# New tables of due times for the planner that orders a fused attention and two-layer feed-forward kernel

## The chip, the cores and the metric

The kernel runs on one core of a Trainium2 chip. The metric is the device time of one execution in microseconds (us), the median of the runs; less is better.

## The reference

Causal attention with a decay bias, then a gated feed-forward layer behind an RMS norm, then a second feed-forward layer, all in fp32. B = 4, H = 8 (32 heads), S = 576, D = 64, 2304 tokens of width 512, inner widths 1536 and 2048.

```python
def _attn_ref(q, k, v, s):
    scores = scale * np.matmul(q, k.transpose(0, 1, 3, 2))
    cum = np.cumsum(np.maximum(s, 0.0), axis=-1)
    bias = -(cum[:, :, :, None] - cum[:, :, None, :])
    scores = np.where(causal, -1000000000.0, scores + np.minimum(bias, 0.0))
    attn = np.exp(scores - np.max(scores, axis=-1, keepdims=True))
    attn = attn / (np.sum(attn, axis=-1, keepdims=True) + 1e-09)
    return np.matmul(attn, v)
...
    # _moe_ref
    xn = x / np.sqrt(np.mean(x * x, axis=-1, keepdims=True) + 1e-06) * rms_g
    g = xn @ w_gate
    return g * (1.0 / (1.0 + np.exp(-g))) * (xn @ w_val) @ w_out
...
    # _moe2_ref
    h = x @ w_in
    return h * (1.0 / (1.0 + np.exp(-1.702 * h))) @ w_out
```

## The kernel before

**Stages.** The attention stage works head by head. `scores(h, u)` is TensorE's product of queries and keys, in five units u; for each block VectorE adds the mask and takes a running minimum (a custom instruction, written to a tile `PA`), and `expo` is ScalarE's exponential with the row sum. `recip` and `norm` divide by the sum (the five `norm` instructions of a head run on GpSimd). `transp(h, t)` is TensorE's transposes of the head, in four runs of 3 or 4, each into one of only two PSUM banks and copied from there by ScalarE or VectorE. `pv(h, piece)` is the product with the values for two heads at once. After the eight heads of a batch, `rms(b)` takes the sums of squares, VectorE works on them in twelve small instructions, and `scale(b, half)` spreads the result by three transposes into a PSUM bank, from where VectorE multiplies it into the tile `xT` in four instructions.

Heads 0 to 13 are multiplied in fp32. Heads 14 to 31 are split into a rounded part and a remainder: for these, `prep` loads Q and K of two heads (two DMAs of 288 KB), rounds, subtracts, and copies the parts to their places by six SBUF-to-SBUF DMAs of 144 KB per head, and two rows of the cumulative bias by one DMA from `ch_d`. All DMAs are issued by SyncE, in one queue.

Into the attention stage two of the twelve inner chunks of the first feed-forward layer are mixed as filler: `fa_tile(j)`, j = 0 to 3, each with 16 groups `gv` of three matmuls (128x384) and four groups `outp` of six. Then comes the **chain**: the rest of both feed-forward layers, by Strassen-like block products, as one chain of TensorE operations of fixed order. The tiles share slots of SBUF by turns; the slot `sd` holds the filler's `FH` first and the chain's block `B21` afterwards, so `B21` can be written only once the last `outp` has read `FH`.

**What sets the order.** Nothing is issued where the code names it. Every operation is recorded with its inputs, outputs and possible engines (`op(eng, fn, ...)`, "AV" for ScalarE or VectorE, "VG" for VectorE or GpSimd). A planner then places all operations: it keeps a model of each engine, takes for each engine the ready operations, and among those the one with the smallest latest start (`alap`). The latest starts are reckoned back from the chain, whose ideal start is the number `TA`, and from due times out of the table `PRM`: `SD` (one number per head for its scores), `HD` (one per pair of heads for `pv`), `FD` (first and last for each filler tile) and `WD` (one for each of the first six weights). They are priorities and not times of day. The planner also picks the engine where there is a choice. The instructions are issued in the order of its starts, and each engine keeps that order (a dependency without a semaphore). Where GpSimd takes an instruction that shares a port with VectorE, it is also made to wait for VectorE's last such instruction.

```python
pick = None
for i in ready[e]:
    t, c = earliest(e, i)
    if t <= tnow and (pick is None or (alap[i], i) < (alap[pick[1]], pick[1])):
        pick = (t, i, c)
```

Since a recording helper issues everything, all rows of the profile show line 211; tiles tell them apart. In the profile's names, `b` is a PSUM bank, `si`, `sk` and some `s` are the `PA` tiles, `sf`, `sg`, `sh` and `sb` the copied transposes, `st` raw weights, and `small` the minima, sums and reciprocals.

Of the kernel before, what the change touches and what calls it, by code (L numbers as in the profile page):

```python
# [39 lines left out]
    "RQ": "AVG", "RV": "VG", "NORM": "G",  # L40
    "SJ": [(2, (2, 3)), (2, (4,)), (1, (2, 3, 4)), (0, (3, 4, 5)), (0, (6, 7)), (1, (5, 6, 7)), (2, (5, 6, 7)),
           (2, (8, 9)), (1, (8, 9)), (0, (8, 9)), (0, (10, 11)), (1, (10, 11)), (2, (10, 11))],
    "HD": [16.92, 309.44, 401.69, 409.67, 394.22, 578.63, 529.92, 440.48, 0.0, 29.27, 423.83, 579.22, 136.47, 502.33, 517.43, 246.34],
    "FD": [(20.84, 419.25), (430.11, 416.77), (419.39, 381.61), (573.39, 343.22)],
    "WD": [636.01, 275.43, 695.53, 257.09, 229.42, 237.34],
    "SD": [331.83, 393.3, 216.64, 633.04, 341.05, 237.85, 481.65, 585.57, 647.63, 420.68, 664.9, 112.11, 264.2, 413.34, 130.04, 443.31, 550.66, 141.32, 470.11, 462.61, 149.18, 360.93, 387.56, 358.59, 700.0, 456.49, 215.88, 71.5, 280.43, 357.78, 664.75, 190.27],
    "TA": 257.35, "REB": 3, "EARLY": False, "MAG": "AV", "PASS": 0, "ISSUE": 0.6, "INNER": 1.0, "IDLE": 3, "PEN": {}, "PVC": (0.81, 2.22),
}


# [1419 lines left out]
```

## Time and profile before

| | |
|---|---|
| median of 3 runs | 1006.09 us (1004.43 to 1006.52) |
| profiled execution | 1007.22 us, span of its profile 1005.4 us |
| TensorE busy | 990.2 us (98%) |
| VectorE, ScalarE, GpSimd busy | 657.4 us (65%), 562.5 us (56%), 272.2 us (27%) |
| TensorE's granted clock | 0.999 of full |

The share of busy time counts a TensorE instruction from its start to its modelled end. The idle time of TensorE is what no instruction covers, and the profile names what released it.

### The profile page before, as it was taken

To read this page: it belongs to the slowest core of one execution; us is meant where nothing else is said; L and a number is where in the kernel's file an instruction comes from. 1 tells how busy PE (TensorE), PEld (TensorE's weight loads), DVE (VectorE), ACT (ScalarE), POOL (GpSimd) and SP (SyncE) were. 2 spreads that over 40 slices of the span, in tenths; PEclk is the share of its full clock that TensorE was granted. 3 is DMA by queue.
4 is the path that set the end of the run, shared out by engine and by line. 5 is a ranking of instruction groups with operands and counts; after the bars stand their busy time and mean duration, and the time that the engine had idled before them with its cause. 6 is when DMAs were issued, how large, how long until landed. Compare 5 with 4: busy or idle time off the path is not lost. (4 is left out here: it accounts for less than half of the span.)

```text
span 1005.4 us, 16237 instructions
## 1 busy us (share of the span) xinstructions
PE 990.2 (98%) x5738; PEld 907.1 (90%) x5738; DVE 657.4 (65%) x1524; ACT 562.5 (56%) x1292; POOL 272.2 (27%) x370
## 2 busy tenths in 40 slices
PE   9999999899999999999999999999999999999998
PEld 6777878789899999999999999999889998899987
DVE  7778786877868887645766858874653565353323
ACT  8999777685566555334444436785643463353322
POOL 5555652442232223002321303231320231020000
PEclk9999999999999999999999999999999999999999
DMA  5347787733676772661484576653276046505541
GB/s 170 96 131 183 192 223 201 178 101 118 251 244 242 267 271 87 260 218 45 132 319 174 209 293 234 275 198 146 88 299 220 22 157 238 192 1 194 212 160 63
DMA packets 62089, 183.49 MB, mean 182 GB/s; under 512 B 7092, under 2 KB 22964, under 8 KB 62008
## 3 DMA queue, kind: packets, MB, share of 16 engines
q1 hardware_dynamic: 62008, 182.46, 53.5%
q8 instruction: 45, 0.74, 0.3%
q14 instruction: 36, 0.29, 0.1%
HBM read 122.32 MB, written 44.19 MB: 166 GB/s over the span
## 5 line engine op out<-in xcount | busy, mean ns | idle before, releaser
L211 ACT ACTIVATE s<-b 128x384 f32<-128x384 f32 (+1 forms) x267 | 127.3, 489 | 145.0 <-PE b L211 82.3
L211 DVE TENSOR_TENSOR xT<-b,xT 128x384 f32<-128x384 f32 (+1 forms) x158 | 92.5, 599 | 87.5 <-PE b L211 86.7
L211 ACT ACTIVATE b<-b 128x384 f32<-128x384 f32 x125 | 58.3, 479 | 107.7 <-DVE b L211 72.3
L211 POOL TENSOR_TENSOR wa<-wa,st 128x512 int32<-128x512 int32 x50 | 66.0, 1319 | 176.0 <-DVE wa L211 83.2
L211 DVE TENSOR_TENSOR s<-b,s 128x384 fp32r<-128x384 f32 (+1 forms) x121 | 66.4, 553 | 68.5 <-ACT s L211 64.1
L211 PE MATMUL b<-s,w 128*128 128x384 f32 x540 | 107.5, 335 | 1.0 <-ACT s L211 0.5
L211 PE MATMUL b<-s 128*128 128x288 f32 (+11 forms) x420 | 101.1, 364 | 4.4 <-DVE small L211 2.2
L211 PEld LDWEIGHTS b<-s,w 128*128 128x128 f32 x540 | 94.9, 188 | 2.8 <-DVE s L211 1.4
L211 PEld LDWEIGHTS b<-s 128*128 128x128 f32 (+1 forms) x420 | 67.1, 192 | 17.7 <-issue 5.3
L211 DVE TENSOR_TENSOR b<-b,s 128x384 f32<-128x384 f32 x82 | 46.1, 562 | 51.6 <-PE b L211 44.0
L211 POOL TENSOR_SCALAR wm<-wm 128x512 f32<-128x512 f32 x68 | 41.8, 615 | 139.6 <-DVE wm L211 46.1
L211 ACT ACTIVATE s<-s,small 128x576 f32<-128x576 f32 (+4 forms) x100 | 55.2, 554 | 13.7 <-DVE small L211 13.1
L211 POOL TENSOR_SCALAR s<-s,small 128x448 f32<-128x448 f32 (+4 forms) x100 | 51.6, 535 | 38.9 <-DVE wm L211 13.9
L211 PE MATMUL b<-sc,w 128*128 128x384 f32 x300 | 61.3, 341 | 0.0
L211 ACT ACTIVATE st<-st 128x512 int32<-128x512 uint32 x68 | 45.8, 674 | 23.7 <-DMA st<-in_w_dram 23.7
L211 PE MATMUL b<-s,s 128*128 128x384 f32 (+1 forms) x252 | 54.9, 346 | 0.0
L211 PE MATMUL b<-sd,w 128*128 128x384 f32 x264 | 52.4, 336 | 0.0
L211 PEld LDWEIGHTS b<-sc,w 128*128 128x128 f32 x300 | 51.4, 188 | 0.3
L211 PE MATMUL b<-w,s 128*128 128x512 f32 x189 | 51.1, 391 | 0.0
L211 PE MATMUL b<-s,sk 128*128 128x384 f32 x246 | 50.7, 335 | 0.0
L211 DVE CUSTOM_DVE_ANT_0 s<-b,s 128x288 f32<-128x288 f32 (+4 forms) x100 | 39.8, 426 | 11.8 <-PE b L211 11.4
L211 PE MATMUL b<-s,sc 128*128 128x384 f32 x228 | 47.2, 334 | 0.0
(265 smaller groups left out, 2375.7 us busy)
## 6 DMA issues: line engine op xcount, KB each, us to landing
st<-in_w_dram SPq DMA_DIRECT2D x68, 512.0 KB
s<-s SPq DMA_DIRECT2D x108, 144.0 KB
xT<-y_d SPq DMA_DIRECT2D x3, 1536.0 KB
s<-pc11B SPq DMA_DIRECT2D x6, 768.0 KB
s<-pc21B SPq DMA_DIRECT2D x6, 768.0 KB
out_dram<-xT SPq DMA_DIRECT2D x18, 256.0 KB
y_d<-se SPq DMA_DIRECT2D x22, 192.0 KB
s<-in_vp_dram SPq DMA_DIRECT2D x16, 256.0 KB
```

The costliest lines, as they stand in the source:

```text
L211: return lambda *args, **kw: f(*[real(x) for x in args], **{k: real(x) for k, x in kw.items()})
```

## The change

Five entries of `PRM` get other numbers: `HD`, `FD`, `WD`, `SD` and `TA`. No code, no tile, no cost of the planner's model and no other entry is changed. One short line of the tables and the line with `TA`:

```diff
-    "WD": [636.01, 275.43, 695.53, 257.09, 229.42, 237.34],
+    "WD": [258.65, 630.56, 454.31, 104.08, 19.12, 583.8],
...
-    "TA": 257.35, "REB": 3, "EARLY": False, "MAG": "AV", "PASS": 0, "ISSUE": 0.6, "INNER": 1.0, "IDLE": 3, "PEN": {}, "PVC": (0.81, 2.22),
+    "TA": 229.72, "REB": 3, "EARLY": False, "MAG": "AV", "PASS": 0, "ISSUE": 0.6, "INNER": 1.0, "IDLE": 3, "PEN": {}, "PVC": (0.81, 2.22),
```

What this does to the order is seen in the built programs. TensorE's operations before the chain stand in another order almost throughout; the order of the chain's own operations is the same, and behind the last norm the rows of all TensorE instructions read alike.

The first place is TensorE at the end of the attention stage: the last filler products (`outp`, tile `sd` by `w`), the transposes of the last norm's first half (`ident,small`), and the chain's products on `B21` (the first tile `sd` by `sl`). Before:

```order
L211 MATMUL b_72<-sd_1339,w_130 128x384 x3
L211 MATMUL b_73<-sd_1339,w_127 128x384 x3
L211 MATMUL b_73<-sd_1339,w_130 128x384 x3
L211 MATMUL b_70<-ident,small 128x128 x2
L211 MATMUL b_70<-ident,small 128x64
L211 MATMUL b_66<-sd_2903,sl_2676 128x384 x6
```

Now:

```order
L211 MATMUL b_73<-sd_1396,w_127 128x384 x3
L211 MATMUL b_73<-sd_1396,w_130 128x384 x3
L211 MATMUL b_67<-s_1_2611,sk_2646 128x384 x6
L211 MATMUL b_70<-ident,small 128x128 x2
L211 MATMUL b_70<-ident,small 128x64
L211 MATMUL b_66<-sd_2882,sl_2735 128x384 x6
```

Six matmuls of the chain (on `sk`) that stood ahead of the filler products now stand behind the last of them.

The second place is SyncE's queue ahead of the scores of head 25: its last part copies (`s_0_928` and `s_0_234`, now `s_0_897` and `s_0_232`, from `s_0_136`), its bias rows (`ch_d`), and the loads of heads 26 and 27 (`in_qT_dram`, `in_kT_dram`). Before:

```order
L211 DMA s_0_928<-s_0_136 64x576 x4
L211 DMA s_0_136<-in_qT_dram 128x576
L211 DMA s_0_928<-s_0_136 64x576
L211 DMA s_0_136<-in_kT_dram 128x576
L211 DMA s_0_234<-s_0_136 64x576
L211 DMA s_0_234<-ch_d 2x576
L211 DMA s_0_149<-in_vp_dram 128x4x128
```

Now:

```order
L211 DMA s_0_897<-s_0_136 64x576 x3
L211 DMA s_0_232<-s_0_136 64x576
L211 DMA s_0_232<-ch_d 2x576
L211 DMA s_0_136<-in_qT_dram 128x576
L211 DMA s_0_136<-in_kT_dram 128x576
L211 DMA y_d<-se_1328 128x384 x2
```

The two loads stood among the copies and ahead of the bias rows; now they stand behind them.

The third place is TensorE around the norm of batch 2: transposes of heads 25 (`s_0_159`), 26 (`s_0_165`) and 27 (`s_0_131`, now), filler (`w`), and the norm's own transposes (`ident,small`; the rows with `x2` and the 64 behind it are the first half, the next three the second). Before:

```order
L211 MATMUL b_69<-ident,s_0_159 128x128 x4
L211 MATMUL b_70<-ident,small 128x128 x2
L211 MATMUL b_70<-ident,small 128x64
L211 MATMUL b_68<-ident,s_0_159 128x128 x4
L211 MATMUL b_69<-ident,s_0_159 128x128 x3
L211 MATMUL b_73<-sc_915,w_129 128x384 x6
L211 MATMUL b_70<-ident,small 128x64
L211 MATMUL b_70<-ident,small 128x128
L211 MATMUL b_70<-ident,small 128x64
L211 MATMUL b_68<-ident,s_0_165 128x128 x4
```

Now:

```order
L211 MATMUL b_68<-ident,s_0_165 128x128 x4
L211 MATMUL b_70<-ident,small 128x128 x2
L211 MATMUL b_70<-ident,small 128x64
L211 MATMUL b_69<-ident,s_0_165 128x128 x3
L211 MATMUL b_73<-sc_925,w_129 128x384 x3
L211 MATMUL b_72<-sc_925,w_128 128x384 x3
L211 MATMUL b_69<-ident,s_0_131 128x128 x4
L211 MATMUL b_68<-ident,s_0_131 128x128 x4
L211 MATMUL b_70<-ident,small 128x64
L211 MATMUL b_70<-ident,small 128x128
L211 MATMUL b_70<-ident,small 128x64
L211 MATMUL b_71<-s_0_897 128x192
```

Head 26's transposes began right behind the second half of the norm; now all but the last run stand ahead of the first half, and two runs of head 27 stand between the halves.

The planner's choice of engine changes too. In the whole program GpSimd gets 13 more two-input instructions (four of 128x576, four of 128x384, three of 128x512, one each of 128x768 and 128x256) and 8 more of 128x5. These 13 leave VectorE, with five one-input roundings and masks; VectorE gets six more copies of 128x448 and one of 128x256 out of PSUM.

## Rows read from the trace of the kernel before

**Rows 1.** The page's head.
```profile
span 1005.4 us, 16237 instructions
```

**Rows 2.** Five stretches: us, then busy us (and instructions) of each engine, clock, DMA.
```profile
0.00:248.00 248.00, 239.94 (x1708) 195.89 (x1709) 191.45 (x663) 197.75 (x562) 123.26 (x225) 1.00 0.59 157
248.00:270.00 22.00, 19.81 (x108) 18.03 (x107) 19.64 (x46) 13.14 (x23) 3.21 (x3) 1.00 0.66 248
270.00:600.00 330.00, 329.07 (x1893) 327.62 (x1893) 230.85 (x439) 159.15 (x317) 78.24 (x77) 1.00 0.59 212
600.00:1000.00 400.00, 399.76 (x2029) 364.60 (x2028) 214.76 (x378) 192.42 (x392) 67.52 (x65) 1.00 0.46 172
1000.00:1005.40 5.40, 1.60 (x8) 0.98 (x6) 0.69 (x1) 0.00 (x0) 0.00 (x0) 0.87 0.26 97
```

**Rows 3.** TensorE's waits from 0 to 270 us: total us, times, longest us.
```profile
PE b L211 <- DVE small L211: 2.2, 4, 1.4
PE b L211 <- POOL s L211: 1.4, 2, 1.3
PE b L211 <- DMA s<-ch_d: 1.4, 1, 1.4
PE b L211 <- DVE xT L211: 0.8, 2, 0.5
PE b L211 <- DVE sg L211: 0.8, 1, 0.8
PE b L211 <- POOL si L211: 0.7, 1, 0.7
PE b L211 <- ACT sd L211: 0.6, 1, 0.6
PE b L211 <- DVE sd L211: 0.5, 1, 0.5
PE b L211 <- DMA s<-s: 0.4, 2, 0.2
PE b L211 <- ACT s L211: 0.4, 1, 0.4
PE b L211 <- DVE sf L211: 0.3, 1, 0.3
PE b L211 <- ACT sg L211: 0.3, 1, 0.3
PE b L211 <- ACT sf L211: 0.2, 1, 0.2
```

**Rows 4.** Timeline at the chain's first products on `sd`: TensorE, ScalarE, VectorE.
```profile
254.84 0.45 PE L211 MATMUL b<-sd,sl 128*128 128x384 f32 x1 [0.57 <-ACT sd L211]
255.83 1.14 PE L211 MATMUL b<-sd,sl 128*128 128x384 f32 x5 [0.55 <-DVE sd L211]
253.94 0.84 ACT L211 ACTIVATE sd<-xT 128x768 fp32r<-128x768 f32 x1 [1.13 <-PE b L211]
254.82 0.96 DVE L211 TENSOR_TENSOR sd<-xT,sd 128x768 fp32r<-128x768 f32 x1
```

**Rows 5.** Timeline of SyncE's queue and TensorE at the scores of head 25.
```profile
162.41 0.54 SPq L211 DMA_DIRECT2D s<-in_qT_dram  x1
...
165.18 0.44 SPq L211 DMA_DIRECT2D s<-ch_d  x1
169.49 1.28 PE L211 MATMUL b<-s 128*128 128x192 f32 x7 [1.43 <-DMA s<-ch_d]
```

**Rows 6.** Timeline of TensorE around the norm of batch 2.
```profile
186.77 0.72 PE L211 MATMUL b<-ident,small 64*128 64x64 f32 x3 [0.51 <-DVE xT L211]
188.76 0.66 PE L211 MATMUL b<-ident,s 128*128 128x128 f32 x4 [1.27 <-POOL s L211]
```

**Rows 7.** Instruction groups from 0 to 250 us: busy us, mean ns.
```profile
L211 POOL TENSOR_TENSOR s<-s 128x576 fp32r<-128x576 f32 x4 | 5.7, 1427 | 5.8 <-DMA st<-in_w_dram 3.5 <-ACT small L211 1.4 <-DVE s L211 0.7
...
L211 DVE TENSOR_TENSOR s<-s 128x576 fp32r<-128x576 f32 x14 | 10.4, 758 | 0.0
```

6 rows, old and new, of the table PRM are left out of this document.

## The prediction

> **What bounds the kernel now.** I read the five stretches first [rows 2]: the granted clock is at its full level (2.4 GHz) in the first four and TensorE is busy nearly throughout. Against the span [rows 1] it is idle for 15.2 us: 8.06 us before 248 us (248.00 - 239.94), 2.19 us to 270 us, 0.93 us to 600 us, 0.24 us to 1000 us, 3.80 us behind that. So TensorE's work is the bound, and another order can give back no more than its idle time. The chain's order is the same in both programs; what lies behind 270 us (4.97 us idle) I leave as it is. The field is the 10.25 us before 270 us.
>
> TensorE's waits in that stretch [rows 3] tell what ends them; the rows add up to 10.0 us. Not all is to be had. The first wait of all, for VectorE's setup (the longest in the first row, 1.4 us), is there in either order. So are the two for `sg` (0.8 + 0.3 us): that block comes from the last norm's second half, and between the two stand the same rows in both orders. This leaves 7.5 us.
>
> **The change, part by part.** The work is the same: the same matmuls, transposes and DMAs. What a term is worth is a wait that the new order takes apart, less what it puts there.
>
> *Filler's end.* `B21` waits for the last filler product to have read the shared slot. ScalarE's half starts at 253.94 us, when TensorE is done with it, and ends at 254.78; VectorE's half runs from 254.82 to 255.78 us, and both halves are waited for, 0.57 + 0.55 us [rows 4]. The new order puts six matmuls of 128x384 between the last filler product and `B21`'s product. One such matmul takes 329.07 / 1893 = 0.174 us in the dense stretch [rows 2], six take 1.04 us. The first product then comes at 254.27 + 1.04 = 255.31 us, behind ScalarE's half; the second, 0.17 us later, meets VectorE's half at 255.83 us and waits 0.35 us. Gain 1.12 - 0.35 = **0.8 us** (0 to 1.1).
>
> *Head 18.* Its transposes wait for GpSimd's division (`si`, 0.7 us) and then run four runs on end through two banks, so that one more waits for ScalarE's copy (`sf`, 0.2 us) [rows 3]. Before, between its last score and its first transposes stood the scores of head 19, one piece of `pv` and two filler groups. In the new order five filler groups of three matmuls (5 x 3 x 0.174 = 2.6 us), two runs and more of other heads' transposes, the norm's second half, the same scores and a shorter piece of `pv` stand there, and two filler products and a piece of `pv` among the runs. The three filler groups more (1.6 us) and the transposes outweigh the longer piece of `pv` by more than the 0.7 us of the wait. Gain **0.9 us** (0 to 0.9).
>
> *Part copies and bias rows.* For head 25 the two bias rows were issued at 165.18 us, behind the loads for the next pair (the first at 162.41 us), and TensorE could go on at 169.49 us, 4.31 us after the issue; it waited 1.43 us [rows 5]. The two waits for part copies (`s<-s`, 0.4 us) are of the same kind (heads 22 and 29), and three of the four for VectorE's `small` (2.2 - 1.4 = 0.8 us) stand next to them [rows 3]: a late score makes the minima late. In the new order head 25's bias rows stand ahead of the loads. Head 29's and head 22's last copies have no load in front of them either. But head 23's bias rows now stand behind the loads of heads 24 and 25, with about as much of TensorE's work between issue and use as head 25 had (from 165.18 us to 169.49 - 1.43 = 168.06 us), so a wait of up to 1.4 us can come back there; I count half. Gain 1.4 + 0.4 + 0.8 - 0.7 = **1.9 us** (0 to 2.6).
>
> *The norm of batch 2.* The second half's transposes wait for VectorE to have read the bank of the first (0.51 us), then head 26's transposes for GpSimd's division, 1.27 us [rows 6], since the division waits for its reciprocal in VectorE's queue behind the eight multiplications into `xT`. In the new order head 26 is transposed ahead of this, and two runs of head 27 and two filler groups stand between the halves: the second wait has lost its cause, and the first shrinks to about 0.2 us, since one run of four transposes more lies between the halves. Gain 1.78 - 0.2 = **1.6 us** (0 to 1.8).
>
> *Norm of batch 0.* Waits of 0.4 us for ScalarE's `s` and 0.3 us for `xT` (what 0.8 leaves beside the 0.51) [rows 3] go. But from head 9 to head 10 the new order has seven runs of transposes on end through two banks. Runs on end cost 0.2 us (`sf`, ScalarE) and 0.3 us (`sf`, VectorE) here [rows 3]; three at 0.25 us take back the 0.7 us. Gain **0** (-1.0 to 0.7).
>
> *Head 27's runs.* The 0.3 us for VectorE's copy [rows 3] goes, since a `pv` and a filler stand between them now. Gain **0.3 us**.
>
> *Engines.* GpSimd takes 13 two-input instructions more. At the row of the largest common kind, 1427 ns [rows 7], that is 13 x 1.43 = 18.6 us at most, in a stretch where it is busy for 123 of 248 us [rows 2]; VectorE, the fuller of the two with 191 of 248 us, gives up at 0.758 us each [rows 7] at most 9.9 us and gets seven copies. I count nothing here: the idle 125 us of GpSimd cover it. Without this cover it is the second rival.
>
> Together 0.8 + 0.9 + 1.9 + 1.6 + 0 + 0.3 = 5.5 us. Against it stand waits that I can't see from the order: TensorE's 409 operations before the chain are shuffled, and any of them can meet an engine that is late. Bounds: 0, and the 7.5 us that the old order has. I take 1.5 us, a fifth, because where I compared them the new distances between a head's scores and its transposes are longer, not shorter. That leaves **4.0 us**. The profiled execution took 1007.22 us, 1.8 us more than its span; 1007.2 - 4.0 = 1003.2. It lies 1.1 us above the median of the runs, so for the median I say 1006.1 - 4.0 = **1002 us**. Of no change 0.2%, 2 us, can be told.
>
> **Rivals.** *Waits only move.* The planner works with its own costs, and what it got wrong in the old order (the bias rows behind the loads) it will get wrong elsewhere: head 23 has that pattern, the seven runs of heads 9 and 10 another. If the new waits add up to 4 to 7 us, the gain is 0 to 1.5 us and the time about 1005.5 us. For it: 7.5 us of such waits in the order before. Against it: no large one is left at the four places that I followed.
>
> *GpSimd becomes late (slower).* Its division stands in one queue with the subtractions. Where a subtraction of 1.43 us stands ahead of a head's five divisions, the head's transposes come late; the wait of 1.27 us in [rows 6] is of that size. If six of the 13 moved instructions do this, they cost 6 x 1.27 = 7.6 us against the 5.5 us gained: 1006.1 + 2.1 = 1008 us. It decides from five on (6.4 us). Against it: half of GpSimd's time is idle. A rule speaks for this rival. In the Trainium skill, the page "SBUF — State Buffer", section "SBUF: two separate sides", says that a VectorE instruction with two SBUF inputs and a GpSimd instruction that reads SBUF can't run together: the one that starts first holds the shared ports to its end. By it each moved subtraction locks VectorE's other two-input work out for 1.4 us instead of taking 0.76 us of VectorE, and the move loses up to 13 x 0.67 = 8.7 us of port time instead of gaining. The trace bears it out only in part: VectorE and GpSimd together are busy for 314.7 us of the 248 us [rows 2], so at least 67 us ran side by side.
>
> *All waits go.* 7.5 us and nothing new: 1006.1 - 7.5 = 998.6 us.
>
> **Chances and range.** The forecast (2 to 6 us gained) 0.50, all waits go (over 6 us) 0.12, waits only move 0.22, GpSimd late or another loss over 2 us 0.16. Faster by over 0.2% is the first two and a little of the third: 0.64; within 0.2%: 0.20; slower: 0.16. The range leaves out a tenth at each end: 998 us, where nearly all waits are gone, to 1008.5 us, where the slower rival decides. The forecast's own range is 1000 to 1004 us.
>
> **What would show it.** What stands at 270 us in the old order comes about 4 us earlier, and everything behind it keeps its length. TensorE's idle time before 270 us falls from 10.25 to about 6 us. There is no wait over 0.5 us for `s<-ch_d` ahead of head 25, none for `POOL` behind the norm of batch 2, and about 0.35 us for `sd`. Head 23 shows a wait for `ch_d` if the pattern of loads is what counts. GpSimd is busy for 10 to 18 us more. It is wrong if waits for GpSimd grow beyond 3 us in all, or if TensorE's idle time before 270 us stays while the places change; or if the chain itself gets longer, which I took as fixed because its order is.

## The result, and the profile after

The changed kernel takes **995.1 us** (median of 4 runs, 994.90 to 995.44) where the kernel before takes 1005.6 us (4 runs, 1004.43 to 1006.52): ratio 0.9897, 95% interval 0.9879 to 0.9914. It is 10.5 us faster. (One later run, of the kernel with the old `WD`, took 1082.06 us at a mean clock of 0.851 and is left out of what follows.) The prediction had the direction, but 1002.0 us and a range that ended at 998 us: the gain is more than twice the 4.0 us of its sum.

The profiled execution took 995.25 us against 1007.22 us. That of the kernel before lay 1.6 us above its median, so about 1.5 us of the difference between the two profiles belong to that execution and not to the change. The head of its page and the busy times, against [rows 1] and the table of the time before:

```profile
span 993.5 us, 16248 instructions
...
PE 985.9 (99%) x5738; PEld 907.2 (91%) x5738; DVE 652.1 (66%) x1513; ACT 563.2 (57%) x1285; POOL 286.7 (29%) x388
```

TensorE has the same 5738 instructions and is busy for 4.3 us less. GpSimd is busy for 14.5 us more (272.2 before), VectorE for 5.3 us less.

To compare like with like I cut both programs where the first pair of products of width 512 (`b` by `w`) begins, in the chain, with the same 1807 matmuls ahead of it. Two stretches of each kernel (columns as in [rows 2]): up to that pair, and from it to the start of the last matmul. Before:

```profile
0.00:268.65 268.65, 258.40 (x1807) 212.66 (x1807) 209.74 (x706) 210.63 (x583) 126.47 (x228) 1.00 0.59 163
268.65:1001.21 732.56, 731.39 (x3933) 694.46 (x3932) 446.97 (x818) 351.82 (x709) 145.76 (x142) 1.00 0.52 190
```

After:

```profile
0.00:257.57 257.57, 254.80 (x1807) 212.70 (x1807) 200.15 (x684) 209.24 (x574) 138.21 (x243) 1.00 0.60 168
257.57:989.24 731.67, 730.73 (x3932) 694.50 (x3932) 451.27 (x829) 353.95 (x711) 148.45 (x145) 1.00 0.52 191
```

The pair comes 11.08 us earlier. Of the span's 11.9 us that leaves 0.9 us behind it: in the chain a wait of 0.51 us for ScalarE's `s` and short stops beside it are gone, and one of 0.69 us for `sf` has come. Ahead of the pair TensorE's idle time fell from 10.25 to 2.77 us, 7.5 us; the other 3.6 us are *busy* time, of the same 1807 matmuls at the same clock. The waits that are left, to be held against [rows 3]:

```profile
PE b L211 <- DVE small L211: 1.4, 1, 1.4
PE b L211 <- DVE sg L211: 0.8, 1, 0.8
PE b L211 <- ACT sf L211: 0.2, 1, 0.2
PE b L211 <- ACT sg L211: 0.2, 1, 0.2
```

Four waits, 2.6 us, instead of 19 with 10.0 us: the setup and VectorE's `sg`, which the prediction said would stay, and two small ones between runs of transposes on end (the other `sg` wait that was to stay, 0.3 us, has no bracket any more). None is for GpSimd or a DMA.

The end of the attention stage on TensorE, ScalarE and VectorE, against [rows 4]:

```profile
244.64 1.68 PE L211 MATMUL b<-sd,sl 128*128 128x384 f32 x6
246.16 1.20 PE L211 MATMUL b<-sd,sk 128*128 128x384 f32 x6
...
252.24 0.43 PE L211 MATMUL b<-sg,w 128*128 128x384 f32 x1
253.47 2.18 PE L211 MATMUL b<-sg,w 128*128 128x384 f32 x11 [0.80 <-DVE sg L211]
...
243.29 0.85 ACT L211 ACTIVATE sd<-xT 128x768 fp32r<-128x768 f32 x1 [1.59 <-PE b L211]
...
244.17 0.96 DVE L211 TENSOR_TENSOR sd<-xT,sd 128x768 fp32r<-128x768 f32 x1 [1.41 <-ACT sd L211]
```

Neither wait for `sd` has a bracket any more. But the six products on `sd` take 1.68 us where the next six take 1.20 us: VectorE's half ends at 245.13 us, and I read the 0.48 us as the wait for it: 0.1 us of it is idle time too short for a bracket, the rest counts as busy. Likewise the single matmul on `sg`, with a wait behind it, counts 0.43 us of busy time; in the dense stretch one takes 0.174 us [rows 2].

Head 25's bias rows on SyncE and its scores, against [rows 5]:

```profile
164.86 0.44 SPq L211 DMA_DIRECT2D s<-ch_d  x1
165.40 0.36 SPq L211 DMA_DIRECT2D s<-in_qT_dram  x1
...
167.94 1.30 PE L211 MATMUL b<-s 128*128 128x192 f32 x8
...
169.88 0.38 PE L211 MATMUL b<-sb,s 128*64 128x192 f32 x1
```

The norm of batch 2 on TensorE, against [rows 6]:

```profile
191.56 0.58 PE L211 MATMUL b<-ident,small 128*128 128x128 f32 x3
...
194.47 0.72 PE L211 MATMUL b<-ident,small 64*128 64x64 f32 x3
```

No brackets at either place.

### The profile page after: what moved, and what is told of

Read it like the earlier page. It is cut to its first block, busy times and chain, and to the rows that moved or that the text cites. A ratio compares the mean times of both kernels' runs of the same rounds, so it can differ in the third digit from the quotient of the medians.

```text
span 993.5 us, 16248 instructions
## 1 busy us (share of the span) xinstructions
PE 985.9 (99%) x5738; PEld 907.2 (91%) x5738; DVE 652.1 (66%) x1513; ACT 563.2 (57%) x1285; POOL 286.7 (29%) x388
## 4 chain that ended last, share of the span: by engine, by line
PE 67%; DVE 1%; ACT 0%; issue 0%
PE b L211 67%; DVE xT L211 0%; DVE s L211 0%; DVE b L211 0%; ACT s L211 0%; DVE sf L211 0%; DVE w L211 0%; ACT wm L211 0%; DVE wm L211 0%; ACT st L211 0%; DVE si L211 0%
## 5 line engine op out<-in xcount | busy, mean ns | idle before, releaser
L211 ACT ACTIVATE s<-s,small 128x448 f32<-128x448 f32 (+4 forms) x100 | 55.1, 553 | 6.9 <-DVE small L211 6.7
```

The source lines that it names most:

```text
L211: return lambda *args, **kw: f(*[real(x) for x in args], **{k: real(x) for k, x in kw.items()})
```

## The experiments

Theory one is the prediction's, with a dearer wait: the new order takes waits apart, and the engine choices count for nothing. Its rival says the engine choices carry the gain. Theory three, set down beside them ahead of the first runs, says that an order is good only with the choices that were planned with it. Beside them stands the question of what a wait costs. Each ratio below is to the kernel before as it ran beside that kernel, with a median of 1006.46, 1007.41 or 1007.30 us; the changed kernel was not run again beside them. The runs are summed up here; "wide pair" is the place of the cut above, waits are those ahead of it, and "lost clock" is the time at half clock there, halved (from windows of 4 or 10 us).

| kernel | median us | wide pair at | TensorE busy to it | waits, us | lost clock |
|---|---|---|---|---|---|
| before | 1005.6 | 268.65 | 258.40 | 19, 10.0 | 0 |
| after | 995.1 | 257.57 | 254.80 | 4, 2.6 | 0 |
| new order, old engines | 1009.40 | 271.45 | 259.81 | 22, 11.0 | 0 |
| old order, new engines | 1022.48 | 283.13 | 265.50 | 24, 17.4 | 3.4 |
| new, 25 VectorE/GpSimd choices back | 999.57 | 261.35 | 256.23 | 11, 5.0 | 0 |
| new, 88 ScalarE/VectorE choices back | 1004.43 | 265.39 | 257.55 | 14, 7.6 | 0 |
| old, loads behind | 1007.30 | 266.53 | 257.71 | 16, 8.5 | 0 |
| old, end moved | 1005.84 | 266.08 | 257.32 | 14, 8.1 | 0 |
| new, loads ahead | 999.17 | 263.18 | 257.54 | 6, 5.5 | 3.4 |
| new, last block later | 995.03 | 256.06 | 254.07 | 3, 1.8 | 0 |
| new, old `TA` | 997.68 | 259.85 | 256.00 | 5, 3.7 | 1.7 |
| new, old `WD` | 994.83 | 256.93 | 254.16 | 4, 2.6 | 0 |
| new, old `SD` | 1008.96 | 272.08 | 261.17 | 16, 10.7 | 3.4 |
| new, old `HD` | 1003.12 | 264.22 | 257.48 | 7, 6.6 | 1.7 |

**Order and engines apart.** The planner of one kernel sets the order, and 132 operations are issued on the engine that the other kernel had for them:

```diff
+    for i, e in {16: "A", 19: "G", 83: "V", ...}.items():
+        chosen[i] = e
```

New order, old engines:

> The new order of all operations, but each of the 132 operations whose engine differs runs on the engine that it had before. Theory one, the order alone takes the waits away: 995 to 997 us against 1005.6 us before, TensorE's bracketed waits before 260 us stay under 3 us. Theory two, the relief of VectorE (13 two-input instructions fewer) does it: most of the gain is lost, 1001 to 1004 us, with new waits of TensorE for VectorE of 4 us or more. Theory three, both must fit each other: near or above the time before, 1003 us or more.

Old order, new engines:

> The old order, with the new engine for the same 132 operations. Theory one (order): no gain, 1004 to 1007 us, the waits of the kernel before stay at their places. Theory two (engines): 997 to 1001 us, the waits behind VectorE (the norm of batch 2, the minima) shrink. Theory three (both must fit): slower than before, 1008 us or more.

Measured: 1009.40 us, ratio 1.0026 (1.0015 to 1.0036), and 1022.48 us, ratio 1.0155 (1.0137 to 1.0173). The longest waits of the first, then of the second:

```profile
PE b L211 <- DVE small L211: 3.4, 7, 1.4
PE b L211 <- DVE sg L211: 2.3, 4, 0.8
PE b L211 <- ACT sb L211: 1.1, 1, 1.1
```

```profile
PE b L211 <- DMA s<-s: 2.9, 3, 1.3
PE b L211 <- POOL si L211: 2.3, 2, 2.1
PE b L211 <- DVE xT L211: 2.1, 2, 1.8
```

Either half alone is slower than the kernel before. Theory one and its rival both fall: the gain belongs to the pair. The next two set back only the choices between VectorE and GpSimd, and only those between ScalarE and VectorE (same edit, shorter lists).

> The new order and engines, but the 25 operations that moved between VectorE and GpSimd are back where they were (19 return to VectorE, 6 to GpSimd). If the relief of VectorE is what makes the new order free of waits: most of the 14 us that all 132 choices cost comes with these 25, 1003 us or more, the waits being for VectorE. If any choice that the planner did not reckon with costs about the same: 25 of 132, that is 2.7 us, 997 to 999 us. If neither matters here: 995 us.

> The new order and engines, but the 88 operations that moved between ScalarE and VectorE (45 and 43, mostly copies of transposes out of PSUM and roundings) are back where they were. If the relief of VectorE by GpSimd counts: little of the 14 us, 995 to 999 us. If the fit of each choice to its place in the order counts: the greater part, 88 of 132 or 9 us and more, 1003 to 1008 us, with waits for both ScalarE and VectorE spread over the attention stage, though the work of either engine is nearly the same in sum.

Measured: 999.57 us, ratio 0.9924 (0.9907 to 0.9941), and 1004.43 us, ratio 0.9971 (0.9958 to 0.9984). They lose 4.5 and 9.3 us; together that is nearly the 14.3 us that all 132 lose (the other 19, which moved between ScalarE and GpSimd, were not set back alone). With VectorE's work given back to it, the waits for its small instructions are there again:

```profile
PE b L211 <- DVE small L211: 2.9, 5, 1.4
```

On average that is 0.18 and 0.11 us for a choice. The loss falls on both kinds and not on one, which speaks for theory three; whether a few single choices carry it was not tried.

**One step of the change at a time.** In the order before, the loads for heads 26 and 27 go behind head 25's bias rows; in the new order, ahead of them. Two rows of the issue order change places, the plan stays:

```diff
+    late = {}
+    at = sorted(range(N), key=lambda i: (start[i], i))
+    for i, j in [(1419, 1380), (1422, 1419)]:
+        at.remove(i)
+        at.insert(at.index(j) + 1, i)
...
-        for i in sorted(range(N), key=lambda i: (start[i], i)):
+        for i in sorted(range(N), key=lambda i: late[i]):
```

> The kernel before, with the two loads for heads 26 and 27 moved behind the bias rows of head 25 in SyncE's queue, nothing else. If the loads ahead of them make the bias rows late: the wait of 1.43 us for ch_d goes or falls under 0.4 us, the bias rows are issued about 1.1 us earlier, and the time falls by 1.4 to 1.7 us to about 1004 us. Rival, the part copies in the queue make them late: the wait stays over 1 us and the time does not move. Second rival, the later loads make head 26 late by as much: the wait goes, another of 1 to 1.5 us comes before head 26 or 27.

> The new kernel with the two loads for heads 26 and 27 moved ahead of head 25's last part copies and bias rows, as they stood before. If loads ahead make the bias rows late: a wait of 1.0 to 2.0 us for ch_d comes before head 25's second product. And the price of a wait: if a bracketed microsecond costs one, the time grows by as much as the bracket; if it costs 1.5 to 1.7, as the six kernels so far suggest, a bracket of 1.4 us costs 2.1 to 2.4 us. If the queue has enough slack here: 995.1 us and no wait.

Measured: in the old order 1007.30 us against 1006.46 us, ratio 1.0010 (0.9997 to 1.0022). In its profile the waits for `ch_d` and `s<-s` are gone and the wide pair comes 2.1 us earlier, but the median shows no gain. In the new order 999.17 us, ratio 0.9917 (0.9895 to 0.9940), 4.1 us lost. TensorE there:

```profile
168.71 0.33 PE L211 MATMUL b<-s 128*128 128x192 f32 x1 [1.10 <-DMA s<-s]
170.82 2.26 PE L211 MATMUL b<-s 128*128 128x192 f32 x7 [1.78 <-DMA y_d<-se]
...
174.34 0.58 PE L211 MATMUL b<-sb,s 128*64 128x192 f32 x1
```

and its windows:

```profile
168.00:172.00 4.00, 1.51 (x6) 1.35 (x7) 0.21 (x1) 0.63 (x3) 0.00 (x0) 0.74 0.56 179
172.00:176.00 4.00, 4.00 (x20) 3.18 (x20) 3.75 (x14) 2.91 (x10) 0.00 (x0) 0.50 0.50 115
```

The waits come back, 2.9 us of brackets where 1.0 to 2.0 us were expected. The profile names a store (`y_d`) for the second; but the products read the bias rows, issued at 166.31 us, and went on 4.5 us later, about as in [rows 5], so I put it down to them. Then the granted clock is at 0.50, the 1.2 GHz level, and a matmul of 192 columns takes 0.58 instead of 0.38 us. The four runs show the two costs apart: at a mean clock of 1.000 they took 996.86 and 997.56 us, 1.8 and 2.5 us more than 995.1 us, which is near what the prediction gave for this step; at 0.997 they took 1000.78 and 1001.79 us.

*Filler's end*, in the order before: the chain's six matmuls on `sk` go behind the last filler product (the same edit, operation 1805 behind 1325).

> The kernel before, with the chain's second group of six matmuls moved behind the last filler product, nothing else. By the prediction's first term: the two waits for sd fall from 1.12 us to about 0.35 us (VectorE's half alone) and the time falls by 0.8 us, to about 1004.8 us. Rival: the wait moves to the tile sg behind the norm's second half, which stands behind the same vector work; the sg wait grows by as much as the sd wait falls and the time stays at 1005.6 us.

Measured: 1005.84 us, ratio 0.9984 (0.9968 to 1.0000), and TensorE's wait for `sd` is as long as it was:

```profile
253.19 1.14 PE L211 MATMUL b<-sd,sl 128*128 128x384 f32 x5 [1.14 <-DVE sd L211]
```

ScalarE's half was done at 251.16 us, but VectorE began its own only at 252.18 us: in the old order one of the norm's multiplications stands ahead of it in VectorE's queue, and that waits for the norm's transposes, which stand behind the six matmuls as well. In the new order the subtraction stands ahead of the multiplications. The wide pair came 2.6 us earlier in this execution, since other waits were shorter: that for head 25's `ch_d` was 0.53 us instead of 1.43 us, though the edit touches nothing there. So one wait for a DMA differed by 0.9 us between two profiles.

The last wait, in the new order: the block that ScalarE and VectorE write for the products behind the wide pair is put behind `sg` and `sf`, so that these come first.

```diff
+    for i, j in [(1826, 1814), (1827, 1815), (1877, 1827)]:
```

> The new kernel with the making of block B21 for the last pair (one ScalarE and one VectorE instruction and the DMA that keeps it) moved behind the blocks in sg and sf, which are needed first. If VectorE's queue makes sg late: the wait of 0.8 us for sg falls under 0.2 us and the time falls by 0.8 to 1.2 us, to about 994.1 us. Rival: B21's products come next and then wait as long, 995.1 us.

Measured: 995.03 us, the same. The wait for `sg` is gone, and one for what was put off comes instead:

```profile
251.88 2.27 PE L211 MATMUL b<-sg,w 128*128 128x384 f32 x12
...
259.97 1.86 PE L211 MATMUL b<-s,sk 128*128 128x384 f32 x9 [0.67 <-DVE s L211]
```

**One table back at a time.** In the changed kernel, each of four tables gets its old numbers (the diff is the line of the change, reversed).

> The changed kernel with the old TA alone. TensorE's order is the same as in the changed kernel row by row; 36 lines of VectorE's order differ, all in the chain. Theory one (the gain is the waits of the attention stage that the new order takes apart): nothing moves there, 995 us, first pair of the chain at about 257.6 us with 4 waits. Rival (the chain got shorter because its ideal start is earlier, which lets its writers go first): up to 0.9 us come back behind the pair, 996 us.

> The changed kernel with the old WD alone: 215 lines of TensorE's order differ. Theory three (each order comes with engine choices that fit it, and a search kept one that fits; a nearby order picked by no search has some of the waits again): a few new waits, 996 to 1000 us. Rival (a few due times of weights do not matter): 995 us. By the price of a wait read so far (its bracket and 0.27 us of busy time more), TensorE's busy time up to the first pair of the chain is 254.8 us plus 0.27 us for each wait beyond 4.

> The changed kernel with the old SD alone (the due times of the scores of the heads): 3265 lines of TensorE's order differ. Theory three (only the tables together give an order whose waits a search has taken out): 12 to 25 waits before the chain, 1002 to 1015 us. Rival (one table carries the gain, and it is not this one): 995 to 998 us. By the price of a wait (its bracket and 0.27 us more), busy time to the first pair of the chain is 254.8 us plus 0.27 us for each wait beyond 4.

> The changed kernel with the old HD alone (the due times of the products with the values): 3352 lines of TensorE's order differ. Theory three: 12 to 25 waits before the chain, 1002 to 1015 us. Rival (one table carries the gain, and it is not this one): 995 to 998 us. Busy time to the first pair of the chain by the price of a wait: 254.8 us plus 0.27 us for each wait beyond 4.

Measured: `TA` 997.68 us, 0.9891 (0.9866 to 0.9916); `WD` 994.83 us, 0.9873 (0.9853 to 0.9893); `SD` 1008.96 us, 1.0009 (0.9995 to 1.0023); `HD` 1003.12 us, 0.9958 (0.9943 to 0.9973). So `WD` is worth nothing, against theory three's 996 to 1000 us, and `HD` gave 7 waits instead of the 12 to 25 expected, though its time lies in the range. With `SD` or `HD` alone set back most or all of the gain is gone. `FD` alone was not tried. No kernel of these is faster than the changed one by more than can be measured.

`TA` was expected to change nothing, and by its order it doesn't: TensorE's rows are the same. In its profile ScalarE has to wait 1.61 us for a DMA out of `se`, `sg` is late, and TensorE stands still twice with one matmul between (ScalarE's row, then TensorE's, then the windows):

```profile
245.99 0.99 ACT L211 ACTIVATE se<-b 128x384 f32<-128x384 f32 x2 [1.61 <-DMA y_d<-se]
```

```profile
252.95 0.44 PE L211 MATMUL b<-sg,w 128*128 128x384 f32 x1 [1.08 <-ACT sg L211]
254.19 3.05 PE L211 MATMUL b<-sg,w 128*128 128x384 f32 x11 [0.80 <-DVE sg L211]
```

```profile
252.00:256.00 4.00, 2.25 (x9) 2.00 (x10) 4.00 (x8) 3.23 (x5) 0.00 (x0) 0.90 0.48 197
256.00:260.00 4.00, 4.00 (x17) 4.00 (x17) 3.41 (x5) 1.34 (x2) 0.45 (x1) 0.67 0.37 152
```

The eleven products behind it take 3.05 us; in the changed kernel they took 2.18 us. Of its four runs three had a mean clock of 0.998 and took 997.60 to 997.82 us, one had 0.999 and took 994.74 us. Whether the old `TA` makes that DMA late or it came so by chance was not shown. The kernel with the old `SD` stands still for 1.42 and 1.83 us at a norm and then has the half clock too:

```profile
199.17 0.63 PE L211 MATMUL b<-ident,small 128*128 128x128 f32 x3 [1.42 <-DVE small L211]
201.63 1.97 PE L211 MATMUL b<-ident,s 128*128 128x128 f32 x8 [1.83 <-POOL s L211]
```

That with `HD` does so behind 2.61 and 0.80 us:

```profile
257.54 0.44 PE L211 MATMUL b<-sg,w 128*128 128x384 f32 x1 [2.61 <-ACT sg L211]
258.78 3.49 PE L211 MATMUL b<-sg,w 128*128 128x384 f32 x11 [0.80 <-DVE sg L211]
```

**The price of a wait.** Take the lost clock off the busy time to the wide pair, and it goes with the number of waits: 254.1 and 254.8 us with 3 and 4 waits, 256.2 us with 11, 257.3 to 257.8 us with 14 to 16, 258.4 us with 19, 259.8 us with 22. A straight line through the fourteen rows has 0.33 us for each wait, and the rows lie about 0.5 us around it; before against after alone gives 3.60 / 15 = 0.24 us. Number and length rise together in these rows, so that number counts more than length is indicated and not shown: a line through the lengths lies about 0.7 us around the rows, and of two rows with nearly the same sum, 11 waits of 5.0 us have 256.2 us of busy time and 6 waits of 5.5 us have 254.1 us.

The starts of the matmuls in the two traces, before and after, say where the 3.6 us lie. I held each distance from one start to the next against the median for the same two neighbours (tiles and shapes) with nothing idle between them, in the nine kernels without lost clock. Beyond its bracket, a wait holds up the matmul just ahead of it by 0.07 to 0.27 us: 2.6 us over 18 waits before (the first wait of all has no matmul ahead), 0.6 us over 3 now. The matmul just behind a wait is longer by 0.9 us in all before and 0.2 us now. Together that is 2.7 of the 3.6 us, or 0.18 us for each of the 15 waits that went. Stops too short for a bracket cost 0.5 us in both. The last 0.9 us lie at no bracketed wait and stay unexplained.

## Why the prediction was wrong

**What failed, by its terms.** The prediction took a wait at its bracket, put the ceiling at the 7.5 us of the waits that could go, counted 5.5 us of them, and took 1.5 us off for waits that it could not see. Its sentence that another order can give back no more than TensorE's idle time is the step that failed first: TensorE is also busy for 4.3 us less. In the profiles, the 4.0 us became 11.9 us by 3.6 us for the price of a wait, 1.9 us for terms set too low (7.4 us of brackets gone for 5.5 us counted), 1.5 us of reserve and 0.9 us in the chain. Measured against that:

- *The price of a wait* is the largest error. The 7.4 us of brackets that went brought 11.1 us at the wide pair. The 3.6 us more are busy time, 0.24 us for each of the 15, of which 0.18 us lie right at the waits. The single matmul ahead of the wait for `sg` shows where it can lie: 0.43 us of busy time instead of 0.174, since nothing follows it within the time to its modelled end. The Trainium skill, page "TensorE: Matmul & The Clock Gate", section "Step-by-step: what each phase is for", says that a matmul with another behind it hides its drain and a single one can't; the trace agrees, with 0.26 us more in that row and, by the starts, 0.07 to 0.27 us lost beyond a bracket. The rival *All waits go* came nearest: with this price its 998.6 us become 998.6 - 3.6 = 995.0 us. That is no test of the price, which was taken from the same two kernels, and it leaves out the chain's 0.9 us.
- *The reserve for unseen waits*, 1.5 us, and the 0.7 us held back for head 23 were not needed. Head 23's bias rows are behind the loads (issued at 152.19 us), but the scores come about 4.4 us later and don't wait. New waits are only the two of 0.2 us.
- *Engines*, counted at nothing, failed as a step although GpSimd's 14.5 us more are covered, as it said: with the old choices the new order gives 1009.4 us. What the order prints as a move on TensorE is worth its waits only if the engines that feed it were chosen for that order. Reading TensorE's and SyncE's order alone could not show this.
- *The chain's length* was taken as fixed; it is 0.9 us shorter, 0.7 us of it busy time, though two waits stand in it as before (0.7 us then, 1.0 us now).

**What held.** *Norm of batch 2*: both waits gone (1.78 us, counted 1.6), but the cause given for the second was half right. The reciprocal was done at 183.50 us; four of the five divisions came late because they stood behind one of GpSimd's own subtractions and then waited 1.08 us for VectorE's `s`, a subtraction that stood behind four of the multiplications. This is the pattern of the rival *GpSimd becomes late*, in the kernel before:

```profile
183.32 0.18 DVE L211 RECIPROCAL small<-small 128x5 f32<-128x5 f32 x1
...
184.97 1.43 POOL L211 TENSOR_TENSOR s<-s 128x576 fp32r<-128x576 f32 x1 [0.74 <-DVE s L211]
187.49 1.94 POOL L211 TENSOR_SCALAR s<-s,small 128x320 f32<-128x320 f32 x4 [1.08 <-DVE s L211]
```

The term came out all the same; with half the cause misread, that was in part luck. *Part copies and bias rows*: all gone (2.6 us, counted 1.9), and putting the loads ahead again brought 2.9 us of waits back; in the old order the same step showed no gain in the median. *Head 18* and *Head 27's runs*: gone (0.9 and 0.3 us). *Norm of batch 0*: gone, and runs on end brought 0.4 us instead of 0.7. *Filler's end*: the 0.35 us left over are there, as 0.48 us inside a row; but the reason was half of it, since the move on TensorE alone left the wait at 1.14 us, and VectorE's order had to change too.

**The rivals.** *Waits only move*: no. *GpSimd becomes late*: no wait for GpSimd is left in the attention stage. The rule that the prediction set beside it (the Trainium skill, page "SBUF — State Buffer", section "SBUF: two separate sides") made the move of two-input work from VectorE to GpSimd a loss of up to 8.7 us; here it went with a gain, and taking the VectorE/GpSimd choices back cost 4.5 us. Whether the lock cost something inside that was not measured.

**What stays open.** Why the medians of the order before scatter by several us, so that 2 us gained in a profile don't show in a median, is only partly told: its runs at a mean clock of 1.000 took 1003.94 to 1007.83 us (8 runs), at 0.998 1006.08 to 1007.94 us (16 runs), and at 0.995 and 0.994 1011.32 and 1012.21 us. The lost clock explains the top of the scatter, not all of it; DMAs that land earlier or later from run to run may be the rest: head 25's wait for `ch_d` was 1.43 us in one profile and 0.53 us in another. That was not shown.

## What to carry to other kernels

On an engine that is busy nearly throughout, the idle time of the profile can fall short of what its waits cost (here 7.5 us for 11.1 us): count the waits as well as their length, and compare two kernels where the same instruction stands, not by busy time. An order out of a planner and its engine choices belong together; a move that looked good on the bounding engine gave nothing here while the queue that feeds it kept the old order (the wait for `sd`), and the whole new order gave nothing with the old engines. Where waits follow each other closely, ask what the clock does behind them before pricing the wait alone.

## What was not expected of the hardware

TensorE's granted clock went to 0.50 behind idle times of 1.10 and 1.78 us with one matmul between (3.4 us lost), 1.42 and 1.83 us (3.4 us lost), 1.08 and 0.80 us (1.7 us lost), and 2.61 and 0.80 us (1.7 us lost). In the profile of the kernel before, 0.51 and 1.27 us close together [rows 6] and 1.43 us alone [rows 5] left it at 1.00. The length of the waits alone doesn't tell when it falls: in the old order with the new engines it fell behind a single wait of 0.67 us, with ten matmuls of 2 columns behind it (1.7 us lost), and behind 1.80 and 1.27 us (1.7 us lost), but stayed at 1.00 behind 2.10 us. So a wait of 2 to 3 us can cost as much again behind it.
